# Pair 3 of step 0 written straight into the tiles of x, step 0's scores in 64-key blocks, GpSimd as a choice for the weights' high parts

## The chip, the cores and the metric

The kernel runs on one core of one Trainium2 chip. The metric is device time in microseconds (us) of one launch; three runs of the kernel before gave 467.01, 467.27 and 467.72, so its median is 467.27 us.

## What is computed

A gated linear attention over 768 positions, 4 batches and 8 heads of 48 values, followed by a two-layer network with a piecewise gate. Cut to what matters:

```python
for t in range(S):
    state = f[t] * state + k[t] (outer) v[t]
    y[t] = q[t] @ state
x = y of all heads, as (B * S, 384)
h = x @ w_in                    # 384 -> 2048
g = where(h >= 1, h, where(h <= -1, 0, (h + 1) ** 2 / 4))
out = g @ w_out                 # 2048 -> 384
```

## The kernel before

The 768 positions are cut into six steps of 128. Heads go in four pairs, and a pair's two heads lie on partitions 0 to 47 and 64 to 111. Per step the attention of the four pairs fills three tiles of x (128 rows by 512 columns, four batches of 128 positions): tile t holds pair t on rows 0 to 47 and 64 to 111, and sixteen of pair 3's values of each head on rows 48 to 63 and 112 to 127. x is kept as a high and a low part in the type fp32r. The network takes a step's x in 16 units; a unit is 9 matmuls of 512 columns into `ph` (L267; `mm_in`), an elementwise chain on ScalarE and VectorE (L270, L273, L278, L934, L281), and 9 matmuls of 512 columns into `po` (L288; `mm_out`). That makes 96 units, u = 0 to 95. The attention of later steps is put between the units: `TURNS` and `VISITS` say after which u a pair is turned, scored, begun and finished, and `AFTER` puts step 0's key transposes (`turn`, `transpose_tensor`, L685) and states after units 0 to 3.

Weights come in as 32 pieces of 128 x 384. `split_piece` (L376 to L393) makes bits on ScalarE (L385), joins them on VectorE (L387), copies the high part (L390 names the choice: ScalarE, and for the first 16 pieces VectorE too), and subtracts it to get the low part on VectorE (L391).

TensorE's instructions stand in the order in which the code adds them. For ScalarE, VectorE, GpSimd and SyncE a planner (`Plan.order`, L98) lists the operations from costs (`COST`) and due times; where `either` gives two engines, it takes the one that it finds free first.

Step 0 has no state before it and is the start of the kernel. Its order is the list `START`: gates of the pairs (L500), their scores (L614), masks (L630), the values times masked scores (`heads`, L851). Pair 3 goes first, in two halves (numbers 3 and 7). In the kernel before, `last` computes pair 3's outputs into a bank of their own (`last_heads`, L853), ScalarE and VectorE round them into a high and a low part (L705, L706, tiles `ghi` and `glo`), and `tile` t brings sixteen rows of each head to rows 48 and 112 of tile t by two matmuls with a selection matrix (L881, `select` made by GpSimd, L844 to L846). `heads` t adds pair t. After that the bank is rounded into x, and `unit_0` (L905) is the first unit's first layer, one third per tile of x. Before START, warm-up matmuls run on zeros (L355).

The scores of step 0 are 128 x 128 per head and batch, all keys by all queries, and a 128 x 128 mask of zeros and ones takes away the later keys. The keys stand in reverse order. The scores of later steps are already taken in 64-key blocks (`scores_of_two`, L666, four 64 x 64 parts of the array at a time).

Of the kernel before, what the change touches and what calls it, by code (L numbers as in the profile page):

```python
# [51 lines left out]
KB_FIRST, KB_LATER, KB_L = 1.75, 0.82, 1.0  # L52
COST = dict(half_dve=350, half_gates=460, half_scores=570, half_log=330, half_sig=330, half_gate=350, gates=870, log=500, mm=227, scores=1100, heads=950, own=1200, tile=680, both=1090, begin=480, before=930, part=560, states=850, parts=830, turn=350, first=110, last=95,
# [4 lines left out]
TURNS = {4: 4, 5: 4, 6: 10, 7: 10, 8: 17, 9: 17, 10: 22, 11: 22, 12: 28, 13: 28, 14: 37, 15: 37, 16: 40, 17: 40, 18: 46, 19: 46, 20: 60, 21: 60, 22: 70, 23: 70}  # L58
VISITS = {4: (4, 5, 6), 6: (10, 11, 13), 8: (21, 22, 26), 10: (26, 27, 29), 12: (28, 32, 37), 14: (37, 39, 40), 16: (40, 45, 47), 18: (47, 60, 61), 20: (61, 69, 70), 22: (70, 75, 77)}
# [3 lines left out]
BY_PRODUCT, ON_EITHER = (), 16  # L63
# [121 lines left out]
def gla_moe(ctx: ExitStack, tc: tile.TileContext, ff, ld, kd, kqd, f0, vv, vl, wd, gates, values, headsd, out):  # L185
# [36 lines left out]
    mask_z = const.tile([C, C + 1], F32, name="mask")  # L222
# [6 lines left out]
    row_ok, least_ok = mask[0:1], ok[0:1, 1:2]  # L229
# [82 lines left out]
    def make_mask():  # L312
        nc.gpsimd.memset(mask_z, 1.0)
        nc.gpsimd.affine_select(out=mask_z, in_=mask_z, pattern=[[1, C + 1]], compare_op=ALU.is_ge, fill=0.0, base=-C, channel_multiplier=1)
# [38 lines left out]
    def warm_first():  # L353
        for cols in WARM:
            nc.tensor.matmul(ph[1][:, 0:cols], zeros, zeros[:, 0:128].rearrange("p (o c) -> p o c", o=1).broadcast_to([128, max(cols // 128, 1), 128])[:, :, 0:min(cols, 128)], start=True, stop=True)  # L355
# [20 lines left out]
    def split_piece(k):  # L376
# [13 lines left out]
        h = plan.either(dict(ACT="part_hi", DVE="cast_384") if k < ON_EITHER else dict(ACT="part_hi"), lambda copy: copy(hi, val), v)  # L390
# [46 lines left out]
    ready = {"mask": set_mask, "sel": add("POOL", 700, make_ident), "mask_t": add("POOL", 600, make_mask_t, set_mask)}  # L437
# [24 lines left out]
    def first_loads(n):  # L462
# [13 lines left out]
        if parts == 1:  # L476
            c["lk"] = 2 * [dma(kq[n][:, 0:2 * N], kd[n], KB_LATER * 512)]
        else:
            c["lk"] = [dma(kq[n][:, a], kd[n, :, a], KB_FIRST * 256) for a in (slice(0, N), slice(N, 2 * N))]
# [122 lines left out]
    def scores(n):  # L602
# [6 lines left out]
        c["held"].append([bank(b) for b in ((5, 6), (3, 4), (5, 2), (3, 4), (5, 6))[n + k * (NP - n)]])  # L609
# [8 lines left out]
    am_of = [am[2:4], kn, am[0:2], am[0:2]]  # L618

    def masks(n):  # L620
# [7 lines left out]
        for h, (b, ps, _) in enumerate(c["held"][k]):  # L628
            t = am_of[n][h]
            o = vec("dve" if parts == 1 else "half_dve", lambda t=t, ps=ps: nc.vector.tensor_tensor(  # L630
                out=t[:, some], in0=ps[:, some], in1=mask.rearrange("u (o t) -> u o t", o=1).broadcast_to([C, B // parts, C]), op=ALU.mult),
                c["sc"][k], ready["mask"], att[3]["y"] if n == 2 else [])
            c["am"].append(o)
            banks[b][:] = [o]
# [43 lines left out]
    def transpose_tensor(n, at=None):  # L678
# [30 lines left out]

    def rounded_by_tensor(b, yf, hi, lo, y):  # L710
        eh = sca("round", lambda: nc.scalar.copy(hi, yf), y)
        banks[b] = [eh]
        return [eh, None]

    def rest(t):

        k, yf, hi, lo = rests[t]
        x = att[NP - 1]["x"] if t == NT else x_of[0, t]
        rows = yf.shape[0]
        o = add("PE", COST["mm"], lambda: nc.tensor.matmul(yf, minus[:rows, :rows], hi, start=False, stop=True), x[0], ready["minus"])  # L720
        x[1] = sca("round", lambda: nc.scalar.copy(lo, yf), o)
        banks[k].append(x[1])
# [112 lines left out]
    sel = glo[0][:R, 0:NT * C].rearrange("r (t c) -> r t c", t=NT)  # L835
    minus = glo[0][:, NT * C:]
    y_last = ghi[1][:R], glo[1][:R]
    rests = {}

    def negative():  # L840
        nc.gpsimd.tensor_scalar(out=minus, in0=ident, scalar1=-1.0, scalar2=None, op0=ALU.mult)

    def select():
        nc.gpsimd.memset(sel.bitcast(F32), 0.0)  # L844
        for t in range(NT):
            nc.gpsimd.tensor_copy(out=sel[:, t].rearrange("r (e c) -> r e c", e=2)[:, :, D:], in_=ident[:R].rearrange("r (e c) -> r e c", e=2)[:, :, 16 * t:16 * t + 16])  # L846

    def heads(n, ps, start, stop):
        for m in range(B):
            for e in range(2):  # L850
                nc.tensor.matmul(ps[64 * e:64 * e + D, m], value(2 * n + e, m), am_of[n][e][:, m], start=start and m == 0, stop=stop and m == B - 1)  # L851

    def last_heads(n):  # L853
        c = att[n]
        b, ps, held = bank(1)
        c["y"] = add("PE", "heads", lambda: heads(n, ps, True, True), c["am"], c["lv"], held)
        if NT in BY_PRODUCT:
            rests[NT] = b, wide(ps)[:R], *y_last
            c["x"] = rounded_by_tensor(*rests[NT], c["y"])
        else:  # L860
            c["x"] = rounded(b, wide(ps)[:R], *y_last, c["y"], None)
# [3 lines left out]
    def half_tile(t, own):  # L865
# [3 lines left out]
        b, ps, held = bank((0, 3, 1)[t])  # L869

        def clear_bank():
            nc.tensor.matmul(wide(ps), zeros, zeros.rearrange("p (o c) -> p o c", o=1).broadcast_to([128, 4, 128]), start=True, stop=False)

        def emit_own():
            if done is None:
                clear_bank()
            heads(t, ps, False, done is not None)

        def emit_last():
            for k in range(2):  # L880
                nc.tensor.matmul(wide(ps), sel[:, t], y_last[k], start=done is None and k == 0, stop=done is not None and k == 1)  # L881

        if own:
            o = c["y"] = add("PE", "own" if done is None else "heads", emit_own, c["am"], c["lv"], held, set_zeros, done)
# [309 lines left out]
```

## Time and profile before

| | |
|---|---|
| median of three runs | 467.27 us |
| the profiled execution | 466.99 us |
| its span, first to last instruction | 465.3 us |
| TensorE busy / VectorE / ScalarE / GpSimd | 458.6 / 345.2 / 299.2 / 24.4 us |
| granted TensorE clock | 1.00 over the whole span |

The span begins with the first instruction and leaves out 1.7 us of the execution's time. In the views, PE is TensorE, DVE VectorE, ACT ScalarE and POOL GpSimd; a line such as L685 is a line of the kernel printed above. An fp32 matmul shows as two instructions (two passes), an fp32 transpose or an fp32r matmul as one. A busy time counts an instruction until its modelled end, so on TensorE, where one begins before the last has ended, the step from start to start is the time that counts.

### The profile page before, as it was taken

How to read it: one execution, taken by the hardware profiler on the slowest of the kernel's cores; microseconds unless marked ns; L12 is line 12 of the kernel's file. 1: busy time of each engine (PE TensorE's matmuls, PEld its weight loads, DVE VectorE, ACT ScalarE, POOL GpSimd, SP SyncE). 2: the span in 40 equal slices, each digit the busy share in tenths (PEclk: the TensorE clock that was granted, in tenths of full speed). 3: DMA queues.
4: the chain of work that ended last, by engine and by line, in shares of the span. 5: the costliest groups of instructions: out<-in, count | busy, mean ns of one | idle time of the engine just before them, and what ended most of it. 6: DMA issues, size and time to landing. Idle time of an engine off the chain costs nothing.

```text
span 465.3 us, 10971 instructions
## 1 busy us (share of the span) xinstructions
PE 458.6 (99%) x4496; PEld 376.2 (81%) x4496; DVE 345.2 (74%) x691; ACT 299.2 (64%) x557; POOL 24.4 (5%) x81
## 2 busy tenths in 40 slices
PE   8999999999999999999999999999999999999996
PEld 5788888888888888888888888888878888888884
DVE  3989987989999998988987887677566755533332
ACT  7799899899574766577576647446536454654443
POOL 4102000010010201000020000000000000000000
PEclk9999999999999999999999999999999999999999
DMA  7888684563023153054236313245412224300001
GB/s 272 296 269 263 210 269 138 187 178 90 4 67 125 49 137 104 1 194 127 59 85 215 117 58 92 68 136 143 132 57 69 71 85 117 102 1 0 1 0 71
DMA packets 21716, 54.19 MB, mean 116 GB/s; under 512 B 3424, under 2 KB 4192, under 8 KB 21664
## 3 DMA queue, kind: packets, MB, share of 16 engines
q1 hardware_dynamic: 21520, 53.37, 36.9%
q8 instruction: 36, 0.59, 0.5%
q10 hardware_dynamic: 144, 0.10, 0.1%
q14 instruction: 16, 0.13, 0.1%
HBM read 44.80 MB, written 4.72 MB: 106 GB/s over the span
## 4 chain that ended last, share of the span: by engine, by line
PE 96%; DMA 2%; SPq 1%; DVE 1%; issue 0%; ACT 0%; DVEq 0%
PE po L288 43%; PE ph L267 42%; PE pa L733 2%; PE pa L755 2%; PE ph L666 2%; DMA kq<-in_k 2%; PE pa L804 1%; SPq L294 1%; PE pa L685 1%; PE pa L666 1%; PE ph L905 0%; PE ph L804 0%; PE pa L783 0%; DVE kq L513 0%; DVE am L630 0%
## 5 line engine op out<-in xcount | busy, mean ns | idle before, releaser
L267 PE MATMUL ph<-x,w_hi 128*128 128x512 f32 x570 | 146.4, 389 | 0.0
L270 ACT ACTIVATE act<-ph,half 128x512 f32<-128x512 f32 x96 | 65.9, 687 | 95.4 <-PE ph L267 94.7
L267 PEld LDWEIGHTS ph<-x,w_hi 128*128 128x128 f32 x570 | 106.9, 188 | 22.2
L278 DVE SCALAR_TENSOR_TENSOR act<-ph,act 128x512 f32<-128x512 f32 x96 | 66.1, 689 | 64.4 <-ACT act L273 63.6
L934 ACT CAST ghi<-act 128x512 fp32r<-128x512 f32 x96 | 59.4, 619 | 50.0 <-DVE act L278 49.7
L288 PE MATMUL po<-ghi,w_hi 128*128 128x512 f32 x288 | 86.2, 401 | 0.0
L288 PE MATMUL po<-ghi,w_lo 128*128 128x512 f32 x288 | 83.2, 390 | 0.0
L288 PE MATMUL po<-glo,w_hi 128*128 128x512 f32 x288 | 82.9, 389 | 0.0
L281 DVE TENSOR_TENSOR glo<-act,ghi 128x512 fp32r<-128x512 f32 x96 | 66.2, 690 | 22.1 <-ACT ghi L934 20.2
L267 PE MATMUL ph<-x,w_lo 128*128 128x512 f32 x285 | 81.6, 389 | 0.0
L700 DVE STREAM_TRANSPOSE kn<-kq 32x128 f32<-32x128 f32 x224 | 67.6, 302 | 3.6
L288 PEld LDWEIGHTS po<-ghi,w_lo 128*128 128x128 f32 x288 | 54.1, 188 | 11.6
L288 PEld LDWEIGHTS po<-glo,w_hi 128*128 128x128 f32 x288 | 54.1, 188 | 11.5
L273 ACT ACTIVATE act<-act 128x512 f32<-128x512 f32 x96 | 60.7, 632 | 2.8
L267 PEld LDWEIGHTS ph<-x,w_lo 128*128 128x128 f32 x285 | 53.5, 188 | 11.1
L288 PEld LDWEIGHTS po<-ghi,w_hi 128*128 128x128 f32 x288 | 52.0, 188 | 11.2 <-ACT ghi L934 0.3
L401 DVE TENSOR_REDUCE ok<-raw 128x1 f32<-128x384 f32 x64 | 33.1, 544 | 2.5 <-DMA raw<-in_w 2.5
L391 DVE TENSOR_TENSOR w_lo<-bits,w_hi 128x384 fp32r<-128x384 f32 x32 | 17.7, 554 | 4.4 <-ACT w_hi L390 3.8
L545 POOL COPY end<-w 128x4 f32<-128x4 f32 x15 | 5.2, 349 | 287.5 <-ACT w L544 287.5
L385 ACT ACTIVATE bits<-raw,top_of 128x384 uint32<-128x384 fp8e4 x32 | 20.1, 645 | 0.0
L596 ACT ACTIVATE sd<-sd,kq 112x48 f32<-112x48 f32 x80 | 19.7, 323 | 0.0
L541 DVE TENSOR_TENSOR_SCAN w<-rec,f 128x512 f32<-128x512 f32 x15 | 18.3, 1219 | 0.8 <-ACT f L540 0.6
(139 smaller groups left out, 382.8 us busy)
## 6 DMA issues: line engine op xcount, KB each, us to landing
raw<-in_w SPq DMA_DIRECT2D x32, 384.0 KB, 3.1
raw<-in_w SPq DMA_DIRECT2D x32, 383.6 KB, 3.6
kq<-in_kq SPq DMA_DIRECT2D x15, 512.0 KB, 4.8
v<-in_v SPq DMA_DIRECT2D x12, 384.0 KB, 3.8
out_y<-raw SPq DMA_DIRECT2D x18, 256.0 KB, 2.5
f<-in_f SPq DMA_DIRECT2D x15, 256.5 KB, 2.9
kq<-kq SPq DMA_DIRECT2D x30, 64.2 KB, 2.6
x<-y SPq DMA_DIRECT2D x30, 64.0 KB, 2.3
```

Of the source, the lines that this page charges most:

```text
L267: nc.tensor.matmul(ps, w_in(w_hi if high else w_lo, j, kt), xt[:, kt, t], start=(n == 0), stop=(n == 8))
L270: nc.scalar.activation(a, ps, AF.Relu, bias=half, scale=0.5)
L273: nc.scalar.activation(a, a, AF.Square)
L278: nc.vector.scalar_tensor_tensor(out=a, in0=ps, scalar=1.0, in1=a, op0=ALU.max, op1=ALU.min)
L281: nc.vector.tensor_tensor(out=lo, in0=a, in1=hi.bitcast(F32), op=ALU.subtract)
L288: nc.tensor.matmul(po[e], w_out(part, j, e), g, start=(j == 0 and n == 0), stop=(j == NJ - 1 and n == 2))
L385: m = sca("bits", lambda: nc.scalar.activation(t, top, AF.Abs, bias=top_of, scale=2.0 ** 30), loaded, made[k - 4] if k >= 4 else None, set ...
L401: seen.append(vec("join", lambda z=z, op=op: nc.vector.tensor_reduce(out=ok[:, 1 + NG + z + c:2 + NG + z + c], in_=words_of(raw[2])[1].bit ...
L541: s1 = vec("scan", lambda: nc.vector.tensor_tensor_scan(out=wide(w), data0=wide(rec), data1=ft[:, N:0:-1], initial=0.0, op0=ALU.mult, op1= ...
L596: nc.scalar.activation(ds[:, at + b * D:at + (b + 1) * D], state[:, p * B + b], AF.Copy, scale=pf[:R, b:b + 1])
L700: nc.vector.transpose(kn[n % 2][to:to + 32, ::-1, r:r + 32], src[:, :, u:u + 32])
L934: o = g["hi"] = sca("copy", lambda: nc.scalar.copy(hi, a), o, unit_out.get(u - 2))
```

## The change

- START has no `last`. `tile` t now multiplies the masked scores of pair 3 with 64 neighbouring columns of the values, such that the last sixteen are the wanted ones, and writes all 64 rows of each half of the bank; `heads` t then overwrites the first 48 of each 64. The selection matrix, the rounding of pair 3 and the clearing of a bank are gone.
- `scores` of step 0 makes, for each batch, the first 64 positions' keys by all 128 queries and the later 64 keys by the later 64 queries. For odd batches the two key halves change places in the bank, so that the long and the short product alternate on the column halves of the array. The value rows of odd batches are exchanged on the host, the mask gets a second version (`make_odd`), and the parts of the banks that are not written hold zeros from the warm-up.
- The key transposes of step 0 follow: for odd batches the transpose of 128 key positions becomes two products of 64 key positions with the identity.
- Pieces 4 and later of the weights may have their high part copied by ScalarE or GpSimd; pieces 0 to 3 by ScalarE or VectorE.
- The order of START, the places in TURNS and VISITS, two costs of scores and the assumed size factor of one load are new.

```diff
-TURNS = {4: 4, 5: 4, 6: 10, 7: 10, 8: 17, 9: 17, 10: 22, 11: 22, ...}
-VISITS = {4: (4, 5, 6), 6: (10, 11, 13), 8: (21, 22, 26), ...}
-START = (("gates", 3), ("gates", 7), ("gates", 0), ("scores", 3), ("scores", 7), ("gates", 2), ("mask", 3), ("mask", 7), ("gates", 1),
-         ("last", 3), ("scores", 0), ("scores", 1), ("tile", 0), ("mask", 0), ("mask", 1), ("heads", 0), ("scores", 2), ("mask", 2), ("tile", 2), ("tile", 1), ("heads", 1), ("heads", 2), ("unit", 0), ("unit", 1), ("unit", 2))
+TURNS = {4: 4, 5: 4, 6: 9, 7: 9, 8: 14, 9: 14, 10: 21, 11: 21, ...}
+VISITS = {4: (4, 5, 7), 6: (9, 10, 11), 8: (17, 21, 24), ...}
+START = (("gates", 3), ("gates", 7), ("gates", 0), ("scores", 3), ("scores", 7), ("mask", 3), ("mask", 7), ("gates", 1), ("gates", 2),
+         ("tile", 2), ("scores", 0), ("tile", 1), ("tile", 0), ("scores", 1), ("mask", 0), ("mask", 1), ("heads", 0), ("scores", 2), ("mask", 2), ("heads", 1), ("heads", 2), ("unit", 0), ("unit", 1), ("unit", 2))
...
+    def make_odd():
+        odd = mask[:, C:]
+        nc.gpsimd.memset(odd[0:T, T:], 1.0)
+        nc.gpsimd.memset(odd[T:, 0:T], 0.0)
+        nc.gpsimd.tensor_copy(out=odd[0:T, 0:T], in_=mask[0:T, T:C])
+        nc.gpsimd.tensor_copy(out=odd[T:, T:], in_=mask[T:, 0:T])
...
-        h = plan.either(dict(ACT="part_hi", DVE="cast_384") if k < ON_EITHER else dict(ACT="part_hi"), lambda copy: copy(hi, val), v)
+        h = plan.either(dict(ACT="part_hi", POOL="pool_hi") if k >= 4 else dict(ACT="part_hi", DVE="cast_384"), lambda copy: copy(hi, val), v)
...
             for m in range(k * B // parts, (k + 1) * B // parts):
-                for (a, z), (_, ps, _) in zip(HEADS, c["held"][k]):
-                    nc.tensor.matmul(ps[:, m], key(n, m)[a:z], query(n, m)[a:z], start=True, stop=True)
+                for half, since in ((1, 0), (0, T)):
+                    at = T * (half ^ m & 1)
+                    for (a, z), (_, ps, _) in zip(HEADS, c["held"][k]):
+                        nc.tensor.matmul(ps[at:at + T, m, since:], key(n, m)[a:z, T * half:T * half + T], query(n, m)[a:z, since:], start=True, stop=True)
...
             for m in range(B):
-                nc.tensor.transpose(ps[:, m, :R], key(p, m)[:R], ident[:R, :R])
+                if i == 0 and m % 2:
+                    for k in range(2):
+                        nc.tensor.matmul(ps[T * (1 - k):T * (2 - k), m, :R], key(p, m)[:R, T * k:T * k + T], ident[:R, :R], start=True, stop=True)
+                else:
+                    nc.tensor.transpose(ps[:, m, :R], key(p, m)[:R], ident[:R, :R])
...
-            for k in range(2):
-                nc.tensor.matmul(wide(ps), sel[:, t], y_last[k], start=done is None and k == 0, stop=done is not None and k == 1)
+            for m in range(B):
+                for e in range(2):
+                    to = (4 * (B + m) + 1 + 2 * e) * D + 16 * (t + 1)
+                    nc.tensor.matmul(ps[64 * e:64 * e + 64, m], v_all[:, to - 64:to], am_of[NP - 1][e][:, m], start=m == 0, stop=m == B - 1)
...
+    vv[0, :, :, 1::2] = np.roll(vv[0, :, :, 1::2], T, axis=1)
```

## Rows read from the trace of the kernel before

**Rows 1.** The page, parts 1 and 2: busy time per engine, TensorE's granted clock.
```profile
PE 458.6 (99%) x4496; PEld 376.2 (81%) x4496; DVE 345.2 (74%) x691; ACT 299.2 (64%) x557; POOL 24.4 (5%) x81
...
PEclk9999999999999999999999999999999999999999
```
**Rows 2.** Chain that ended last, 20 to 33 us: start, us, what, count.
```profile
20.42 2.30 PE ph L905 x9
22.72 0.39 PE pa L685 x4
23.11 0.38 PE po L685 x4
23.49 2.08 PE ph L267 x9
...
30.74 0.77 PE pa L685 x8
```
**Rows 3.** The same chain, 50 to 60 us, around one visit.
```profile
50.56 2.04 PE ph L267 x9
52.60 1.04 PE pa L755 x64
53.64 0.45 PE pa L733 x32
54.09 2.27 PE po L288 x9
56.36 2.04 PE ph L267 x9
```
**Rows 4.** The same chain, the load that the start waits for.
```profile
4.68 7.12 DMA kq<-in_k
```
**Rows 5.** Timeline of VectorE in the start: start, us, operation, idle before.
```profile
11.89 0.69 DVE L512 TENSOR_TENSOR kq<-kq,raw 112x512 f32<-112x512 f32 x1 [0.92 <-DMA kq<-in_k]
12.50 0.68 DVE L513 TENSOR_TENSOR kq<-kq,raw 112x512 f32<-112x512 f32 x1
13.10 0.68 DVE L706 TENSOR_TENSOR glo<-pa,ghi 112x512 fp32r<-112x512 f32 x1
13.70 0.68 DVE L630 TENSOR_TENSOR am<-po,mask 128x512 f32<-128x512 f32 x1
...
15.49 0.69 DVE L513 TENSOR_TENSOR kq<-kq,sd 112x512 f32<-112x512 f32 x1
...
18.36 0.68 DVE L630 TENSOR_TENSOR am<-pa,mask 128x512 f32<-128x512 f32 x1
```
**Rows 6.** Timeline of TensorE in the start.
```profile
10.68 1.08 PE L851 MATMUL pa<-am,v 128*48 128x128 f32 x16 [0.36 <-DMA v<-in_v]
...
13.23 1.16 PE L614 MATMUL po<-kq 48*128 48x128 f32 x16 [0.39 <-DVE kq L513]
...
17.32 0.50 PE L881 MATMUL pa<-ghi,glo 112*128 112x512 f32 x1
...
18.47 1.08 PE L851 MATMUL po<-kn,v 128*48 128x128 f32 x16
19.38 1.04 PE L851 MATMUL pa<-am,v 128*48 128x128 f32 x16
20.35 0.50 PE L905 MATMUL ph<-x,w_lo 128*128 128x512 f32 x1
```
**Rows 7.** Groups by line and shape: the copies of high parts, and GpSimd's nearest work.
```profile
L390 ACT CAST w_hi<-bits 128x384 fp32r<-128x384 f32 x26 | 13.1, 505 | 1.6 <-DVE bits L387 1.6
...
L390 DVE CAST w_hi<-bits 128x384 fp32r<-128x384 f32 x6 | 2.2, 359 | 0.2
...
L841 POOL TENSOR_SCALAR glo<-ident 128x128 fp32r<-128x128 f32 x1 | 0.5, 532 | 0.1
...
L846 POOL CAST glo<-ident 112x32 fp32r<-112x32 f32 x3 | 0.5, 209 | 0.1
```
**Rows 8.** Timelines of GpSimd and VectorE at 153 us.
```profile
153.82 1.52 POOL L545 COPY end<-w 128x4 f32<-128x4 f32 x1 [17.49 <-ACT w L544]
...
154.01 0.69 DVE L546 TENSOR_TENSOR kq<-kq,w 128x512 f32<-128x512 f32 x1
154.61 0.69 DVE L547 TENSOR_TENSOR kq<-kq,f 128x512 f32<-128x512 f32 x1
```
**Rows 9.** Busy time of each engine by stretch (columns as named), 20 to 100 us.
```profile
20.00:100.00 80.00, 80.00 (x903) 65.64 (x900) 70.46 (x127) 73.43 (x148) 3.71 (x10) 1.00 0.69 218
```
**Rows 10.** Timeline, 43 to 45 us: a weight piece's high part and its first use.
```profile
43.74 0.52 ACT L390 CAST w_hi<-bits 128x384 fp32r<-128x384 f32 x1
...
44.78 1.07 PE L267 MATMUL ph<-x,w_hi 128*128 128x512 f32 x4
```

More of the change, by code (lines that the diff above doesn't have):

```diff
@@ L51 @@
 HOP, LANDING, PER_KB, NEAR, ADDING, PATIENCE, FLAG_BY = 200, 2200, 3.0, 3500, 1500, 0, 60000
-KB_FIRST, KB_LATER, KB_L = 1.75, 0.82, 1.0
-COST = dict(half_dve=350, half_gates=460, half_scores=570, half_log=330, half_sig=330, half_gate=350, gates=870, log=500, mm=227, scores=1100, heads=950, own=1200, tile=680, both=1090, begin=480, before=930, part=560, states=850, parts=830, turn=350, first=110, last=95,
+KB_FIRST, KB_NEXT, KB_LATER, KB_L = 1.75, 1.21, 0.82, 1.0
+COST = dict(pool_hi=800, half_dve=350, half_gates=460, half_scores=440, half_log=330, half_sig=330, half_gate=350, gates=870, log=500, mm=227, scores=840, heads=950, own=1200, tile=680, both=1090, begin=480, before=930, part=560, states=850, parts=830, turn=350, first=110, last=95,
@@ L221, in gla_moe @@
     w_lo = const.tile([128, NW, W], F32R, name="w_lo")
-    mask_z = const.tile([C, C + 1], F32, name="mask")
+    mask_z = const.tile([C, 2 * C + 1], F32, name="mask")
     mask = mask_z[:, 1:]
@@ L312, in make_mask @@
     def make_mask():
-        nc.gpsimd.memset(mask_z, 1.0)
-        nc.gpsimd.affine_select(out=mask_z, in_=mask_z, pattern=[[1, C + 1]], compare_op=ALU.is_ge, fill=0.0, base=-C, channel_multiplier=1)
+        causal = mask_z[:, 0:C + 1]
+        nc.gpsimd.memset(causal, 1.0)
+        nc.gpsimd.affine_select(out=causal, in_=causal, pattern=[[1, C + 1]], compare_op=ALU.is_ge, fill=0.0, base=-C, channel_multiplier=1)
     def make_ident():
@@ L353, in warm_first @@
     def warm_first():
-        for cols in WARM:
-            nc.tensor.matmul(ph[1][:, 0:cols], zeros, zeros[:, 0:128].rearrange("p (o c) -> p o c", o=1).broadcast_to([128, max(cols // 128, 1), 128])[:, :, 0:min(cols, 128)], start=True, stop=True)
+        for k, cols in enumerate(WARM):
+            nc.tensor.matmul((po + ph)[k if k < 4 else 4][:, 0:cols], zeros, zeros[:, 0:128].rearrange("p (o c) -> p o c", o=1).broadcast_to([128, max(cols // 128, 1), 128])[:, :, 0:min(cols, 128)], start=True, stop=True)
     add("PE", 3700, warm_first, set_zeros)
@@ L630, in masks @@
             o = vec("dve" if parts == 1 else "half_dve", lambda t=t, ps=ps: nc.vector.tensor_tensor(
-                out=t[:, some], in0=ps[:, some], in1=mask.rearrange("u (o t) -> u o t", o=1).broadcast_to([C, B // parts, C]), op=ALU.mult),
-                c["sc"][k], ready["mask"], att[3]["y"] if n == 2 else [])
+                out=by_two(t[:, some]), in0=by_two(ps[:, some]), in1=mask.rearrange("u (o t) -> u o t", o=1).broadcast_to([C, B // 2 // parts, 2 * C]), op=ALU.mult),
+                c["sc"][k], ready["odd"], att[3]["y"] if n == 2 else [])
             c["am"].append(o)
@@ L708, in rounded @@
         return [eh, el]
[L710 to L722, printed above, removed]
     def attended(n, other):
@@ L831, in states_by_parts, with heads @@
         freed(k, held, o, z)
[L835 to L848, printed above, removed]
+    def heads(n, ps):
         for m in range(B):
             for e in range(2):
[L851 to L861, printed above, removed]
+                nc.tensor.matmul(ps[64 * e:64 * e + D, m], value(2 * n + e, m), am_of[n][e][:, m], start=m == 0, stop=m == B - 1)
     half_of = {}
@@ L868, in half_tile @@
         done = half_of.get(t)
[L869 to L877, printed above, removed]
+        b, ps, held = bank((0, 2, 1)[t])
         def emit_last():
[L880 to L881 removed]
+            for m in range(B):
+                for e in range(2):
+                    to = (4 * (B + m) + 1 + 2 * e) * D + 16 * (t + 1)
+                    nc.tensor.matmul(ps[64 * e:64 * e + 64, m], v_all[:, to - 64:to], am_of[NP - 1][e][:, m], start=m == 0, stop=m == B - 1)
         if own:
[L884 to L890 removed]
+            o = c["y"] = add("PE", "heads", lambda: heads(t, ps), c["am"], c["lv"], done)
+            x_of[0, t] = rounded(b, wide(ps), x[0][:, t, 0], x[0][:, t, 1], o, None)
+        else:
+            o = add("PE", "heads", emit_last, d["am"], d["lv"], held)
+            d.setdefault("y", []).append(o)
+            half_of[t] = o
     gs, left = {}, {}
@@ L995, in gla_moe @@
         att[n]["lv"] = att[n - 1]["lv"]
-    ready["ident"] = ready["sel"]
-    ready["sel"] = add("POOL", 1200, select, ready["ident"])
-    ready["minus"] = add("POOL", 1500, negative, ready["ident"])
-    work = dict(gates=first_gates, mask=masks, scores=scores, last=last_heads, heads=lambda t: half_tile(t, True), tile=lambda t: half_tile(t, False), rest=rest, unit=unit_0,
+    work = dict(gates=first_gates, mask=masks, scores=scores, heads=lambda t: half_tile(t, True), tile=lambda t: half_tile(t, False), unit=unit_0,
                 turn=lambda n: transpose_tensor(n, {0: 1, 1: 5}.get(n)), states=lambda n: states(n))
@@ L1161 @@
     f0 = f0.reshape(128, NG)
-    vv = np.ascontiguousarray(v[:, heads].reshape(B, 2, 4, NI, C, D)[:, :, :, :, ::-1].transpose(3, 1, 4, 0, 2, 5))
+    vv = np.array(v[:, heads].reshape(B, 2, 4, NI, C, D)[:, :, :, :, ::-1].transpose(3, 1, 4, 0, 2, 5), order="C")
+    vv[0, :, :, 1::2] = np.roll(vv[0, :, :, 1::2], T, axis=1)
     w = moe_w_in.reshape(H, D, DF)
```

22 lines of the change are left out of this document (9 added, 13 removed).

## The prediction

> **What bounds the kernel now.** I read the page's busy times first, then the chain of work that ended last, then the timelines of the stretch where that chain isn't TensorE. TensorE is busy for 99% of the span, at the full clock of 2.4 GHz throughout [rows 1]. In the chain it works without a gap from 20.42 us on: unit follows unit in 2.04 us for nine matmuls, and what stands between them is attention [rows 2, 3]. So the span has two parts. After 20.42 us only the amount of TensorE's work counts, changes of its array's shape included. Before 20.42 us it waits, and what counts is how soon the first unit can begin.
>
> That start hangs on one load and then on VectorE. The keys and queries of pair 1 leave SyncE at 4.68 us and land 7.12 us later, at 11.79 [rows 4]. VectorE has stood idle for 0.92 us by then, and from there it works back to back, one 512-column operation each 0.60 us: gating pair 1, the rounding of pair 3 (13.10), masks of pair 0, gating pair 2 (ending at 16.18), masks of pairs 1 and 2, the last ending at 19.04 [rows 5]. TensorE follows it: scores of pair 2 after 16.18, selection matmuls for two tiles (from 17.32), heads 1 at 18.47, heads 2 at 19.38, first unit at 20.35 [rows 6].
>
> **The start, part by part.** Removed from the path: the rounding of pair 3, 0.60 us of VectorE right after the awaited load [rows 5], its copy on ScalarE, and six selection matmuls. Added: `tile` three times instead of `last` once, each eight products of two passes like a `heads`, which takes 0.9 us from start to next start (18.47 to 19.38) [rows 6]. The scores get three quarters of their columns, since the long and short blocks fill the two column halves in turn: 1.16 us in the view less a pipeline end, 0.85 of it streaming [rows 6], so about 0.2 less for each.
>
> I lay the new order on the old landings. The loads are issued in nearly the same order, since what decides their due times keeps its order; only the gate logits of pairs 1 and 2 change places. `tile` 2 needs the values, as `last` did, so it starts at 10.68. Scores 0 then run from 11.7, tile 1 from 12.55, tile 0 from 13.4, scores 1 from 14.4 to 15.15, heads 0 from 15.25, scores 2 from 16.25 to 17.0, heads 1 from 17.2 to 18.07. VectorE from 11.89: two operations of pair 1's gates, two masks of pair 0 (until 14.3), two gates of pair 2 (15.5), two masks of pair 1 (16.7), the joining of a weight piece in the gap, two masks of pair 2 from 17.25, ending at 18.53. Heads 2 waits for that, runs from 18.6 to 19.5, and the first unit starts at 19.6 instead of 20.35: **0.75 us sooner**. If VectorE is no obstacle, TensorE's own sum gives 19.05, a gain of 1.3; if the planner puts another operation or two ahead of a mask, it gives 0 to 0.15. I take 0.75, because rows 5 show VectorE without a gap in this stretch. Next late would be the mask of pair 2, as now.
>
> Of work at no cost: GpSimd makes the second mask instead of the selection matrix, of about as much work, and has nothing else to do then (24.4 us of work in all [rows 1]); if it came late, the masks of pair 3 would wait, ahead of the load at 11.79. The warm-up has the same columns, only other banks. Units read the same x.
>
> **The key transposes.** This term isn't hidden by anything, for it lies after 20.42. Now eight transposes of two pairs take 0.77 us, one each 0.096 us, and the unit behind them takes 2.08 instead of 2.04 [rows 2]: they use the whole array, as units do. In the change, two of the four transposes of each of the four pairs become two products on 64 columns of the array each. Each is fp32 with two passes; the halves run beside each other, as the heads e = 0 and 1 do (16 passes of 128 columns in 0.9 us, [rows 6]), so an odd batch streams 0.19 us instead of 0.096. That is 8 x 0.095 = 0.76 us. Then the array changes its shape twice for each odd batch, since even and odd ones alternate. Rows 3 price one such change and back: the first attention group takes 1.04 us for 64 passes where the next takes 0.45 for 32, so 0.14 us to go in; the group of nine behind takes 2.27 instead of 2.04, so 0.23 to come out, of which 0.04 is there after transposes too [rows 2, 3]. I take 0.14 + 0.19 = 0.33 for each of eight. In sum 8 x (0.095 + 0.33) = **3.4 us added**. Bounds: 0.76 if a change between small products costs nothing, 8 x (0.285 + 0.37) = 5.2 if the halves don't overlap either.
>
> **GpSimd and the weights.** Pieces 4 to 31 may have their high part copied by GpSimd, and as ScalarE is busy for 73.4 of the 80 us from 20 to 100 [rows 9], the planner will give it most. That frees some 28 x 0.45 us of ScalarE and a little of VectorE, which is worth nothing while TensorE has no gap. Its price is not in the trace. The nearest rows are a cast of 32 columns in 0.21 us and an operation on 128 in 0.53 [rows 7], which go on to 1.4 us for 384; the columns of the plain copies would give 0.9. ScalarE's takes 0.505. A piece is made just ahead of its use: one is copied by 44.26 and used at 44.78 [rows 10]. Against a delay of 0.4 to 0.9 stand that 0.5 and the 2.65 us by which TensorE is later from unit 2 on, so I cost it at nothing; this cover is gone if the transposes turn out free, and then a few tenths for each tight piece come back. The upper end is a rival below.
>
> The new places: the visits fall on 24 different units before and 24 after, so the changes of shape there stay the same in number, and with no gap on TensorE their place is free.
>
> **Sum.** The profiled execution took 466.99: -0.75 + 3.4 gives 469.64. The median of the three runs is 0.28 above it: **469.9 us**. The terms' bounds give 466.99 - 1.3 + 0.76 = 466.5 and 467 + 5.2 = 472.2 on the profiled execution.
>
> **The rivals.** First, **the transposes cost only their columns**: TensorE takes the changes of shape in its stride because no wait stands there, and only 0.76 us is added. For it: no row has whole-array and half-array products alternate so finely. Against it: 2.27 follows every visit I looked at [rows 3]. With the start at TensorE's own limit this gives 467.27 - 1.3 + 0.76 = 466.7, not slower. It decides from 0.07 us per change and back: below that, 8 x (0.095 + 0.07) = 1.3 is paid by the start. Chance 0.17. A start much sooner still (masks of pair 0 and gates of pair 2 in the wait for the load), with cheap transposes, would give 466 or below; chance 0.08.
>
> Second, **GpSimd and VectorE block each other**. A copy of four elements on GpSimd took 1.52 us while VectorE ran operations with two inputs from SBUF back to back, VectorE's own taking their usual 0.69 [rows 8]. VectorE makes the low part in its order and would stand waiting for a copy that it held up itself. VectorE has 80 - 70.5 = 9.5 us free from 20 to 100 [rows 9], so it decides at about 9.5 / 28 = 0.34 us lost per copy; at 0.6, some 7 us are lost on VectorE beyond that and perhaps 5 reach TensorE: 469.9 + 3 to 5, near 474. Chance 0.12. The Trainium skill, SBUF — State Buffer, section "SBUF: two separate sides", says that GpSimd and a VectorE operation with two SBUF inputs share one pair of ports, that whichever starts first has it for its whole instruction, and that the other is blocked. By that rule a 1 us copy would also hold VectorE, up to 28 us in all; the trace agrees for the one direction, GpSimd held, and no row shows the other.
>
> Third, the start doesn't move, because another wait (the values of pairs 0 and 1, the second such load) or the planner's order on VectorE takes the place: 466.99 + 3.4 + 0.28 = 470.7. I count it with the forecast.
>
> **How the numbers follow.** Forecast with its variants (start 0 to 1.3 sooner, transposes 2 to 5): 0.63, which is slower. GpSimd blocking: 0.12, slower. Cheap transposes: 0.17, within 0.2% (0.93 us, about what a measurement of this kernel can tell from no change). A much sooner start: 0.08, faster. So faster 0.08, same 0.17, slower 0.75. The range from 466.6 to 472.2 holds the forecast's bounds and most of the first rival, and leaves out the blocking and the sooner start.
>
> **What would show it.** Right, if the chain has the first unit (L905) at 19.3 to 19.9 us, if two step-0 turns take 1.5 to 1.9 us instead of 0.77 with the half-array products in separate lumps, and if nine-matmul groups still follow at 2.04 and 2.27. Wrong, if the turns take under 1.2 us, if the first unit is under 19.0 or over 20.3, or if TensorE's groups show idle time released by VectorE's low parts or GpSimd's copies between 25 and 100 us; GpSimd's busy time there divided by its copies gives their price.

## The result and the profile after

The changed kernel takes 470.29 us (median of six runs, 469.81 to 470.88) beside 467.35 us for the kernel before on the same chip (six runs, 467.01 to 468.14): a ratio of 1.006, with a 95% interval from 1.0047 to 1.0073. It is slower by 2.9 us. The profiled execution took 470.04 us with a span of 468.3, against 466.99 and 465.3.

In the page of after, the first line of part 1 answers to [rows 1]. TensorE is busy for the same 99%, with 116 more matmuls in the records; its granted clock is at the upper level in all 40 slices, as before.

```profile
PE 461.8 (99%) x4612; PEld 377.2 (81%) x4612; DVE 347.0 (74%) x688; ACT 295.7 (63%) x545; POOL 32.0 (7%) x93
```

The chain that ended last, of the kernel after, from the last work of the start to the second unit (it answers to [rows 2]; columns: start, us, what, count; L841 is `heads`, L878 the first unit's first layer, L700 the half-array products and L702 the whole transposes of step 0's turns):

```profile
18.15 0.21 PE ph L358
18.37 1.26 PE pa L841 x16
19.62 2.30 PE ph L878 x9
21.93 0.10 PE pa L702
22.02 0.34 PE pa L700 x4
22.36 0.24 PE pa L702
22.61 0.34 PE pa L700 x4
...
24.13 2.27 PE ph L266 x9
...
29.52 2.04 PE ph L266 x9
```

The first unit begins 0.80 us sooner (19.62 against 20.42). Then two turns take 2.20 us (21.93 to 24.13) where they took 0.77, and the unit behind them 2.27 instead of 2.08. A whole transpose that begins the turns shows 0.10, one behind half-array products 0.24: that is the way back, 0.14 to 0.15. An odd batch (four instructions, two products of two passes) takes 0.34 where, standing among others of its kind, it takes 0.19 (shown with the sorted batches below): about 0.15 to go in. The other two turns, at 31.56, look the same.

So that kernels can be compared whatever their start, I took the starts of the units from the timeline of TensorE, counted from the start of the first unit, and the end of the span counted from the last matmul's start (us). "Unit 3" lies behind all turns of step 0, "unit 95" is the last.

| kernel | first unit at | unit 1 | unit 3 | unit 5 | unit 95 | end after last matmul |
|---|---|---|---|---|---|---|
| before | 20.35 | 2.91 | 13.09 | 24.43 | 432.03 | 4.75 |
| after | 19.55 | 4.50 | 16.32 | 27.65 | 435.57 | 5.05 |
| difference | -0.80 | +1.59 | +3.23 | +3.22 | +3.54 | +0.30 |

The sum is -0.80 + 3.54 + 0.30 = +3.04, the 3.0 us of the span. From unit 5 to unit 95 only 0.3 is added: 0.4 at one place, a turn of a later step at 69 us, less 0.1 that comes back later. In the timeline of TensorE (start, us, operation, idle before and its releaser):

```profile
69.58 0.57 PE L702 MATMUL pa<-ident,kq 112*128 112x112 f32 x4 [0.20 <-DVE w_lo L398]
```

The view counts idle time from the modelled end of the work before, so it shows 0.20 of the 0.4. It names VectorE's low part, which ended at 69.51, but the records speak for a load. The keys of this turn (pair 3) are put in place by a transfer `kq<-kq` (L296), issued at 64.00 and landed at 69.38, and the turn begins 0.20 us behind that. When the same kernel was run again, the transfer landed at 69.78 and the turn began at 69.98, while that low part ended only at 70.08. With all copies on GpSimd it landed at 67.68, and the turn didn't wait.

The last 0.30 is the landing of the last output, which came between 4.75 and 5.96 us after the last matmul in the fourteen profiles of this case. The two lowest values are those of the kernel before and of the split alone in it; the changed kernel has 5.05 here and 4.85 when run again, so two executions of one kernel differ by 0.20 there.

GpSimd got 13 of the 28 copies that it might have had. From the groups by line and shape, of GpSimd and of ScalarE (they answer to [rows 7]), and the busy times from 20 to 100 us (they answer to [rows 9]):

```profile
L397 POOL CAST w_hi<-bits 128x384 fp32r<-128x384 f32 x13 | 9.5, 734 | 44.3 <-DVE bits L394 44.3
...
L397 ACT CAST w_hi<-bits 128x384 fp32r<-128x384 f32 x19 | 9.6, 509 | 1.5 <-DVE bits L394 1.3
```
```profile
20.00:100.00 80.00, 79.80 (x907) 63.79 (x906) 71.13 (x122) 70.34 (x136) 14.10 (x25) 1.00 0.69 215
```

ScalarE lost 3.1 us of work in that stretch (73.43 to 70.34), VectorE gained 0.7, and TensorE still has next to no idle time.

### The profile page after: what moved, and what is told of

Same layout as the page of the kernel before. It is cut to its first block, busy times and chain, and to the rows that moved or that the text cites. A ratio compares the mean times of both kernels' runs of the same rounds, so it can differ in the third digit from the quotient of the medians.

```text
span 468.3 us, 11210 instructions
## 1 busy us (share of the span) xinstructions
PE 461.8 (99%) x4612; PEld 377.2 (81%) x4612; DVE 347.0 (74%) x688; ACT 295.7 (63%) x545; POOL 32.0 (7%) x93
## 4 chain that ended last, share of the span: by engine, by line
PE 95%; ACT 1%; DVE 1%; DMA 1%; issue 0%; SPq 0%; DVEq 0%
PE po L287 42%; PE ph L266 41%; PE pa L736 2%; PE pa L758 2%; PE ph L679 2%; DMA kq<-in_k 1%; PE pa L807 1%; PE pa L841 1%; PE pa L855 1%; PE po L623 1%; PE pa L702 1%; PE pa L679 1%; PE ph L878 0%; PE pa L507 0%; PE pa L700 0%; PE ph L807 0%
## 5 line engine op out<-in xcount | busy, mean ns | idle before, releaser
L280 DVE TENSOR_TENSOR glo<-act,ghi 128x512 fp32r<-128x512 f32 x96 | 67.4, 703 | 22.4 <-ACT ghi L907 20.6
```

The costliest lines, as they stand in the source:

```text
L280: nc.vector.tensor_tensor(out=lo, in0=a, in1=hi.bitcast(F32), op=ALU.subtract)
```

## The experiments

Each kernel was timed against the kernel before on the same chip. Differences of single places are taken from the profiles, by the table's measure.

**The split transposes alone, in the kernel before.** Nothing else of the change is made.

```diff
-                nc.tensor.transpose(ps[:, m, :R], key(p, m)[:R], ident[:R, :R])
+                if i == 0 and m % 2:
+                    for k in range(2):
+                        nc.tensor.matmul(ps[T * k:T * k + T, m, :R], key(p, m)[:R, T * k:T * k + T], ident[:R, :R], start=True, stop=True)
+                else:
+                    nc.tensor.transpose(ps[:, m, :R], key(p, m)[:R], ident[:R, :R])
```

> The kernel before with one thing alone: step 0's key transposes of odd batches as two half-array products. Theory (the changes of the array's shape and the extra columns make the loss): 8 odd batches at about 0.40 us, so 3.2 us more, 470.6 against 467.35; the first unit stays at 20.4 us, and two turns take 2.2 us instead of 0.77. Rival (the loss of the change comes from GpSimd's copies or the new places): 467.4, at most 0.8 us more for the extra columns.

Measured: 470.91 us against 467.69, ratio 1.007 (1.0053 to 1.0087). Unit 3 comes 16.30 us behind the first unit, 3.21 later than in the kernel before. The chain shows the same steps as that of after (here L687 are the half-array products, L689 the whole transposes):

```profile
23.13 0.10 PE pa L689
23.23 0.34 PE pa L687 x4
23.57 0.24 PE pa L689
...
25.34 2.27 PE ph L267 x9
```

These eight split transposes alone make the loss: 3.2 us on TensorE, and 3.2 on the median.

**The batches sorted.** In the changed kernel, the whole transposes of two pairs stand together, and the half-array ones too. The work is the same, only the number of changes of shape falls.

```diff
-            for m in range(B):
+            for m in (range(B), (0, 2, 1, 3), (1, 3, 0, 2))[0 if i else 1 + n % 2]:
```

> The changed kernel with the batches of each two turns sorted as 0, 2, 1, 3 and 1, 3, 0, 2, so that the four half-array batches stand together: one change of shape and back for two turns instead of four. Theory (0.31 us per change and back, 0.095 us of columns per odd batch): two turns take 0.92 us less, in sum 1.85 us less, 468.4 against 470.3. Rival (the half-array products themselves are that slow, wherever they stand): no difference, 470.3.

Measured: 468.47 us against 467.69, ratio 1.0019 (1.001 to 1.0028); the changed kernel itself has 1.006. Unit 3 comes 14.41 us behind the first unit instead of 16.32, so 1.91 is saved. The chain:

```profile
22.82 0.19 PE pa L702 x2
23.02 0.53 PE pa L700 x8
23.55 0.38 PE po L700 x8
23.93 0.34 PE po L702 x2
24.27 2.08 PE ph L266 x9
```

Two turns now take 1.45 us, and the unit behind them 2.08: together 0.66 more than with whole transposes, where the changed kernel pays 1.60. Both pay the same columns, four odd batches of 0.095, which is 0.38. What is left is 1.22 for four changes and back, 0.31 each, and 0.28 for the single one here. So the shape change is the larger part of the price, 2.5 us of the 3.2 for all eight. The rival, half-array products that are slow wherever they stand, falls: in a lump four odd batches' products add only their columns (two batches in 0.38).

**Whole transposes, the halves exchanged by the copy out.** The transposes are as before, and the copy of step 0's turned keys becomes three, of which two exchange the key halves of the odd batches.

```diff
-                if i == 0 and m % 2:
...
+                nc.tensor.transpose(ps[:, m, :R], key(p, m)[:R], ident[:R, :R])
...
+                copy(kn[n % 2][:, 0::2, :R], ps[:, 0::2, :R])
+                copy(kn[n % 2][0:T, 1::2, :R], ps[T:C, 1::2, :R])
+                copy(kn[n % 2][T:C, 1::2, :R], ps[0:T, 1::2, :R])
```

> The changed kernel with whole transposes for all batches; the copies out of the bank, three instead of one for each pair of step 0, put the halves of odd batches in their places. Theory: TensorE gets back 3.2 us, two turns take 0.77 us again, the first unit stays at 19.55 us: 467.1, so 0.2 to 0.6 us below the kernel before if the earlier start is a gain by itself. Rival (the pieces of weights or the states come late once TensorE is that much sooner, so that the start's gain goes into a wait in units 0 to 3): 467.4 or above, with idle time on TensorE before the states.

Measured: 468.48 us against 467.69, ratio 1.0026 (1.0014 to 1.0038). The turns are back at their old cost: unit 3 comes 13.05 us behind the first unit. But a weight's high part is now late by the time that TensorE has come sooner. From the timelines of ScalarE and TensorE:

```profile
38.64 0.49 ACT L397 CAST w_hi<-bits 128x384 fp32r<-128x384 f32 x1
...
39.19 1.20 PE L266 MATMUL ph<-x,w_hi 128*128 128x512 f32 x4 [0.55 <-ACT w_hi L397]
```

In the kernel after, a copy begins at 38.70 too, and TensorE doesn't wait there. Unit 5 is 25.49 us behind the first unit, where the kernel before has 24.43, so 1.06 is lost again, which is more than the start has gained. The rival held in kind, a weight that is late, though behind the states and not ahead of them.

**The same, with all copies of high parts from piece 4 on given to GpSimd.**

```diff
-        h = plan.either(dict(ACT="part_hi", POOL="pool_hi") if k >= 4 else ...
+        h = plan.either(dict(POOL="pool_hi") if k >= 4 else ...
```

> Whole transposes and exchange by the copies, as in the run that had a late weight piece at 38 us, and all high parts from piece 4 on by GpSimd. Theory (ScalarE was what made the piece late): no gap at 38 us, the start's 0.75 us stay, 0.5 to 0.8 us below the kernel before. Rival (the pieces stay late, now by GpSimd or the loads): a gap of 0.5 us or more in units 2 to 6, no faster than the kernel before.

Measured: 468.49 us against 467.42, ratio 1.0023 (1.0013 to 1.0033). The rival held, and the waits only move: unit 5 comes 25.73 us behind the first unit, 1.30 later than in the kernel before. Ahead of unit 5 the view has one wait of 0.4 us, put down to VectorE's low part; the rest is in shorter waits, which it leaves out:

```profile
PE po L287 <- DVE w_lo L398: 0.4, 1, 0.4
```

**The same again, with the old places of TURNS and VISITS.** The diff sets the two dictionaries back to the lines taken out in the change.

> The same with the places of the kernel before. Theory (with GpSimd making the high parts the plan has no gap at either set of places): equal to the run before it within 0.3 us. Rival (the new places belong to the new plan): 0.5 us or more slower than it, with a gap at one of the visits.

Measured: 471.28 us against 467.42, ratio 1.0094 (1.0068 to 1.0121). The rival held. With the old places TensorE falls behind the kernel before in the stretches from 128, 159 and 201 us, by 1.0, 0.5 and 1.4; unit 95 comes 436.29 us behind the first, 2.5 later than with the new places (433.78). The profiled execution of this kernel was 3.2 us above its median, with a late first unit (22.58), so only its places are used here.

**The exchange left out.** The turns are whole and the copy out is the single old one, all else is as in the kernel after.

```diff
-                if i == 0 and m % 2:
-                    for k in range(2):
...
-                else:
-                    nc.tensor.transpose(ps[:, m, :R], key(p, m)[:R], ident[:R, :R])
+                nc.tensor.transpose(ps[:, m, :R], key(p, m)[:R], ident[:R, :R])
```

> The changed kernel with whole transposes and one copy out of the bank as before. Left out: the exchange of the key halves of step 0's odd batches, so the states after step 0 are of other numbers; work and waits are otherwise the kernel's. Theory (the late weight piece of the two runs with three copies comes from the two additional copies on ScalarE and VectorE): no gap on TensorE up to unit 5, which begins 24.4 us after the first unit, 0.5 to 0.8 us below the kernel before. Rival (the weights are made no sooner, so a sooner start has to wait for them): unit 5 begins 25.0 us or more after the first unit, and the time is within 0.4 us of the kernel before.

Measured: 467.13 us against 467.33, ratio 1.0002 (0.9992 to 1.0012). The chain has the early start and the old turns, and later the copy of the outputs before the last transfer:

```profile
19.63 2.30 PE ph L874 x9
21.93 0.39 PE pa L698 x4
22.31 0.38 PE po L698 x4
22.70 2.08 PE ph L266 x9
...
460.14 0.58 ACT raw L933
```

No weight is late: unit 5 is 24.43 and unit 95 is 432.02 us behind the first unit, as in the kernel before. This kernel and the kernel after differ in the split transposes alone, and unit 95 comes 3.55 us sooner here, 3.23 of it by unit 3: with the split alone in the kernel before, that shows from both sides what the loss is. It also shows that the waits of the three experiments above came with the two added copies and the plan around them, not with an earlier TensorE alone. TensorE ends 0.80 sooner (the output's copy begins at 460.14 instead of 460.95), yet the median is only 0.2 lower, which is not clear of the noise and misses the 0.5 to 0.8 expected. In the one profile the last output landed 0.92 us later behind the last matmul (5.67 against 4.75), which takes up the gain. The three output transfers took 2.50, 2.52 and 2.99 us there, and 2.17 to 2.19 in the kernel before; in the changed kernel run again they took 2.17 to 2.28, so the longer ones don't belong to the new start as such. One profile doesn't settle whether they always take the gain; this stays open.

**Whole scores.** In the kernel after, step 0's scores, mask and transposes are as before, with no exchange at all; pair 3 still goes straight into the tiles.

```diff
-                for half, since in ((1, 0), (0, T)):
-                    at = T * (half ^ m & 1)
...
+                for (a, z), (_, ps, _) in zip(HEADS, c["held"][k]):
+                    nc.tensor.matmul(ps[:, m], key(n, m)[a:z], query(n, m)[a:z], start=True, stop=True)
...
-    vv[0, :, :, 1::2] = np.roll(vv[0, :, :, 1::2], T, axis=1)
```

> The changed kernel with step 0's scores whole again, 128 keys by 128 queries, and so without exchanged halves, second mask or split transposes; pair 3 still goes straight into x. Theory (TensorE's own work from the first tile to the last scores sets the start, and each scores costs 0.17 us more): first unit at 20.0 us, 467.5. Rival (VectorE's chain of gates and masks sets the start, the blocks are worth nothing): first unit at 19.6 us, 467.1.

Measured: 467.59 us against 467.69, ratio 1.0003 (0.9992 to 1.0014). The whole loss is gone, and the start's gain too. The values landed later on this chip (the first product of pair 3 began at 11.12 instead of 10.64), so I compare from that product on. From it to the first unit the kernel before takes 9.68 us (10.68 to 20.35 [rows 6]), this one 9.65 (11.12 to 20.77), and the kernel after 8.91. The timeline of TensorE in the kernel after, for that:

```profile
10.64 1.09 PE L855 MATMUL pa<-am,v 128*64 128x128 f32 x16
...
14.40 0.90 PE L623 MATMUL po<-kq 48*64 48x128 f32 x32
15.23 1.08 PE L841 MATMUL pa<-am,v 128*48 128x128 f32 x16
...
17.07 1.08 PE L841 MATMUL pa<-kn,v 128*48 128x128 f32 x16
18.08 0.28 PE L358 MATMUL ph<-zeros 128*128 128x256 bf16 x1
18.30 1.33 PE L841 MATMUL pa<-am,v 128*48 128x128 f32 x16
19.55 0.50 PE L878 MATMUL ph<-x,w_lo 128*128 128x512 f32 x1
```

The scores of pair 1 take 0.83 us from start to next start (14.40 to 15.23); whole ones take 1.09 in the experiment (15.13 to 16.22). Three times 0.26 is 0.78, about the 0.74 between the two kernels. Writing pair 3 straight into the tiles alone buys nothing: the scores of pair 2 begin 6.11 us behind the first product instead of 5.55, because of the three `tile` groups, and from there to the first unit it takes 3.54 instead of 4.12. The other half alone, blocks in the kernel before, wasn't run, so the experiment doesn't say that the blocks would bring 0.74 without the other edit.

**The changed kernel again**, on the chip of the next three experiments:

> The changed kernel as it is, on the same chip as the next three. Theory: first unit 8.9 us after the first tile's matmuls begin, two turns 2.2 us, 2.6 to 3.0 us above the kernel before. The wait of 0.39 us of the turn of pair 3 in step 1 (at 69 us in the profile after) is a late landing and comes and goes: 0 or 0.4.

Measured: 470.86 us against 467.58, ratio 1.0065 (1.004 to 1.0091), 3.3 us above the kernel before where 2.6 to 3.0 was expected. The first unit begins 9.10 us behind the first tile's matmuls (seven of the eleven profiles of this start have 8.91), two turns take 2.20 us, and the turn at 69 us loses 0.2, between the two values expected.

**The old places in the changed kernel.** TURNS and VISITS are set back, nothing else.

> The changed kernel with the TURNS and VISITS of the kernel before. Theory (with no gap on TensorE the places are free): within 0.4 us of the changed kernel. Rival (the new places bring waits): 0.5 to 1 us faster than it.

Measured: 473.13 us against 467.58, ratio 1.0115 (1.0093 to 1.0137), 2.3 us over the changed kernel: neither the theory nor the rival held. Unit 95 comes 1.55 later behind the first unit (437.22 against 435.67 in the changed kernel run beside it), and in two places the plan has put matmuls on zeros into gaps that it expected; whether TensorE would really have waited so long there isn't shown. One of the two, in the timeline of TensorE:

```profile
159.22 0.82 PE L353 MATMUL po<-zeros 128*128 128x512 bf16 x3
```

Such matmuls stand nowhere behind the start of the kernel after. The other stands at 375.69. The profiled execution also has a later landing of the last output (5.96 against 4.85 us behind the last matmul).

**No copies on GpSimd.** The choice of engines for the high parts is the old one.

```diff
-        h = plan.either(dict(ACT="part_hi", POOL="pool_hi") if k >= 4 else dict(ACT="part_hi", DVE="cast_384"), ...
+        h = plan.either(dict(ACT="part_hi", DVE="cast_384") if k < 16 else dict(ACT="part_hi"), ...
```

> The changed kernel with the high parts copied as before, by ScalarE or, for the first 16 pieces, VectorE. Theory (GpSimd's 13 copies cost and bring nothing while TensorE is later by 2.4 us): within 0.4 us of the changed kernel. Rival (GpSimd and VectorE block each other to TensorE's loss): 1 us or more faster.

Measured: 474.66 us against 467.58, ratio 1.0149 (1.0126 to 1.0173), 3.8 us over the changed kernel; again neither held. Unit 95 comes 438.66 us behind the first, 3.0 later. The largest gap is the same turn at 70 us: its transfer `kq<-kq` was issued at 66.48 instead of 64.00 and landed at 71.70, 0.24 before the turn (the view names another load). About 1.2 us more are four matmuls on zeros that the plan put at 105 us, and 0.4 more is lost at about 149 us, where masked scores are late. From the timeline of TensorE, and the busy times from 20 to 100 us:

```profile
71.94 0.57 PE L702 MATMUL pa<-ident,kq 112*128 112x112 f32 x4 [1.05 <-DMA raw<-in_w]
```
```profile
20.00:100.00 80.00, 78.95 (x909) 62.62 (x905) 66.19 (x119) 69.75 (x140) 3.74 (x9) 1.00 0.65 203
```

**All 28 copies on GpSimd.** The diff is that of the run "with all copies given to GpSimd", made in the kernel after.

> The changed kernel with all 28 high parts of pieces 4 to 31 on GpSimd. Theory: a copy takes 0.50 us alone and 0.8 beside VectorE, VectorE's operations with two inputs lose up to 0.3 each, some 6 to 8 us in sum, which its idle time until 100 us takes in: at most 0.5 us slower than the changed kernel. Rival (the loss reaches TensorE): 3 to 5 us slower, with TensorE waiting for low parts between 25 and 100 us.

Measured: 470.36 us against 467.58, ratio 1.0057 (1.0037 to 1.0077), 0.5 below the changed kernel and within the spread of four runs each; the theory held. From the groups, and the busy times from 20 to 100 us:

```profile
L397 POOL CAST w_hi<-bits 128x384 fp32r<-128x384 f32 x28 | 19.9, 717 | 51.7 <-DVE bits L394 51.7
```
```profile
20.00:100.00 80.00, 80.00 (x907) 64.12 (x908) 72.17 (x121) 65.16 (x125) 25.83 (x40) 1.00 0.70 218
```

The view shows no idle time of TensorE behind the start, not even at 69 us, although GpSimd does more than twice the copies.

**Old places and old engines together**, both of the last diffs in the kernel after.

> The changed kernel with both the places and the choice of engines for high parts of the kernel before. Theory (places and engines have to fit each other; the loss of the change itself is the split transposes): TensorE has under 1 us of gaps and fillers after the first unit, 470.3 to 471.2. Rival (the changed start needs GpSimd's help with the weights, wherever the visits are): 472 or more, with TensorE waiting between 60 and 110 us.

Measured: 473.54 us against 467.42, ratio 1.013 (1.0109 to 1.0151). Unit 95 comes 438.39 us behind the first, 2.7 later than in the changed kernel, so the rival's time came. Of its waits, at 69.7, 130.8 and 379 us, only the first lies where the rival put it, and at 161 us the plan has three matmuls on zeros. TensorE's waits behind the start:

```profile
PE pa L736 <- DVE am L685: 0.6, 1, 0.6
...
PE po L287 <- ACT ghi L907: 0.3, 1, 0.3
...
PE po L287 <- ACT w_hi L397: 0.3, 1, 0.3
```

In the kernel before the two old parts leave TensorE no gap, and with the split transposes alone they cost 0.45 (unit 95 at 435.69, less 3.21 for the turns, against 432.03). With the new start they don't fit. Which of its shifted operations on ScalarE and VectorE makes the difference wasn't tried.

## Why the prediction was right, and where its reasons weren't

**The key transposes** were the largest term and held: 3.4 us forecast, 3.23 measured in the kernel after and 3.21 with the split alone. The columns were right (eight times 0.095 us, from halves that run beside each other). The change of shape and back was put at 0.33 from [rows 3]; the two kernels with and without sorting give 0.31 and 0.28. Its parts lie a little otherwise, about 0.15 to go in and 0.14 to come out where another attention product follows, and 0.19 more than after whole transposes in the unit behind the last one (2.27 against 2.08).

**The first rival**, that only columns are paid, needed less than 0.07 us per change and falls with that.

**The start** had the right size, 0.75 forecast and 0.80 measured, and the steps that I laid out came near: scores of pair 2 at 16.24 (16.25 in the forecast), heads 2 at 18.30 (18.6), the first unit at 19.55 (19.6). The last masks, in the timeline of VectorE in the kernel after (it answers to [rows 5]):

```profile
16.67 0.55 DVE L394 SCALAR_TENSOR_TENSOR bits<-raw,bits 128x384 uint32<-128x384 uint32 x1
17.20 0.69 DVE L643 TENSOR_TENSOR am<-po,mask 128x512 f32<-128x512 f32 x1
17.81 0.68 DVE L643 TENSOR_TENSOR am<-ph,mask 128x512 f32<-128x512 f32 x1
```

They end at 18.49, as forecast (18.53), and heads 2 waits for them, as forecast. With 0.91 us for heads 1 from 17.07 and 0.97 for heads 2 (their steps in [rows 6]), the first unit would begin at 18.95 without that wait (19.05 in the forecast) instead of 19.55; the matmul on zeros at 18.08 only fills part of it.

The step that failed is where the gain was booked: "Removed from the path: the rounding of pair 3, 0.60 us of VectorE right after the awaited load". With rounding and selection gone but whole scores, the start gains nothing (9.65 against 9.68); with the 64-key blocks added it gains 0.74 more, 0.26 for each of three scores where I took 0.2. Yet the removal isn't idle. In the kernel before, the chain comes to the scores of pair 2 from VectorE's gate:

```profile
15.49 0.70 DVE kq L513
...
16.23 0.37 PE po L614
```

In the kernel after, that gate ends at 15.56, and TensorE's own work sets when these scores begin, at 16.24. So in the kernel before, shorter scores ahead of that gate would have met a wait, and only the 0.26 of pair 2's would be left, an estimate from these rows that no run tested. The two edits seem to need each other; I had laid out one sum with both in it, and that its size came out doesn't confirm the share given to either.

**GpSimd's copies.** The step "the planner will give it most" failed: it gave 13 of 28. The price of a copy was too high: 0.9 to 1.4 us was extrapolated from smaller operations, and a copy that nothing holds up takes 0.50. The cover for late pieces was put too early, too: it was to be 2.65 us from unit 2 on, but only two of the four turns are done by then, and TensorE is 0.8 us later at unit 2 and 2.4 from unit 3 on. Costing the copies at nothing was wrong in its reason, since "worth nothing while TensorE has no gap" holds only as long as the plan around them has no gap either: without them the new plan loses 3.0 us on TensorE, 1.2 of it in matmuls on zeros that the plan itself put in. Since they come together with the plan that needs them, the sum was not hurt.

**The blocking rival** decided at 0.34 us lost on VectorE per copy, and would have cost 3 to 5 us. VectorE lost less: in the kernel after, eight of its operations that met a copy took 2.1 us more in all than such operations take otherwise, 0.16 per copy, and with all 28 copies fourteen took 3.8 us more, 0.14 per copy, without idle time on TensorE. The copies themselves took 0.23 longer on average (734 ns against 0.50). The blocking itself is there, in both directions. From the timelines of GpSimd and VectorE in the kernel after:

```profile
35.57 0.90 POOL L397 CAST w_hi<-bits 128x384 fp32r<-128x384 f32 x1 [0.75 <-DVE bits L394]
...
89.64 0.51 POOL L397 CAST w_hi<-bits 128x384 fp32r<-128x384 f32 x1 [7.31 <-DVE bits L394]
...
95.56 1.37 POOL L397 CAST w_hi<-bits 128x384 fp32r<-128x384 f32 x1 [3.37 <-DVE bits L394]
```
```profile
35.42 0.68 DVE L553 TENSOR_TENSOR kq<-kq,w 128x512 f32<-128x512 f32 x1
36.02 0.99 DVE L280 TENSOR_TENSOR glo<-act,ghi 128x512 fp32r<-128x512 f32 x1
...
89.80 0.89 DVE L280 TENSOR_TENSOR glo<-act,ghi 128x512 fp32r<-128x512 f32 x1 [0.22 <-ACT ghi L907]
...
95.42 1.22 DVE L548 TENSOR_TENSOR_SCAN w<-rec,f 128x512 f32<-128x512 f32 x1
```

The copy at 35.57 begins inside L553 and takes 0.90; the next operation with two inputs, L280, begins inside the copy and takes 0.99 where its mean over the kernel is 0.70. The copy at 89.64 begins ahead of L280 and keeps its 0.51, and L280 takes 0.89. So the copies of 0.50 are not all alone: most of them began first. The Trainium skill, SBUF — State Buffer, section "SBUF: two separate sides", says that whichever of the two starts first holds the shared ports for its whole instruction, and that the other is blocked. The trace now agrees in the direction that no row before showed, VectorE held by GpSimd, at 0.2 to 0.3 us for an operation that met a copy. What the rival had wrong is the price of a meeting, and that VectorE had the time for it.

**The new places** were called free: "the visits fall on 24 different units before and 24 after ... their place is free". That failed as a reason. Their changes of shape do cost the same (with whole transposes unit 95 comes at 432.03 with the old places and at 432.02 with the new), but the places also decide when ScalarE and VectorE must have the attention's operations done. The old places cost the changed kernel some 1.5 us on TensorE, in gaps and in matmuls on zeros. The forecast was not hurt, because the new places suit the new plan, which I had not shown.

**The third rival**, a start that doesn't move, falls with the 0.80, and so does a much sooner start with cheap transposes. What the sum did not hold is 0.31 between units 5 and 95, from the turn at 69 us (0.4 there in this profile, 0.2 when the kernel was run again), and 0.30 at the last transfer. With the start 0.05 and the transposes 0.17 below their terms, that makes the 0.4 by which the profiled execution (470.04) lies above the sum (469.64); that the errors lay on both sides is luck.

**The signs.** The first unit (19.62 in the chain, 19.3 to 19.9 expected) and the groups of nine at 2.04 and 2.27 came as named. The range for two turns, 1.5 to 1.9 us, was a slip: the prediction's own terms give 0.77 + 4 x 0.425, less the 0.19 paid in the unit behind, which is 2.28, and 2.20 was measured; 1.70 is only what is added. One sign of being wrong showed up in small, idle time of TensorE put down to VectorE's low part (0.20 at 69 us); as laid out above, it goes back to the landing of a transfer.

## What to carry to other kernels

When TensorE has no gap, it can pay to sort small products by the part of the array that they use: here the same eight split transposes cost 3.2 us one by one between whole ones and 1.3 us in lumps. Before a second benefit is booked for an edit that stands next to another, one should ask by which of the two it would be lost; here the one edit alone brought nothing, both together brought 0.77 us of the start, and the other alone wasn't run. Places and engine choices of a planned kernel are tuned together, and a part that "costs nothing" in one plan costs 2 to 4 us when it is put into another.

## What the runs showed of the hardware that was not expected

GpSimd copied 128 x 384 from fp32 to fp32r in 0.50 to 0.51 us in 7 of 13 copies, as fast as ScalarE (0.509). The other six began while a VectorE operation ran, and took 0.77 to 0.90, or 1.37 beside a scan. In eight cases a VectorE operation that began inside a copy took 0.2 to 0.3 longer.

Two batches of half-array fp32 products in a lump took 0.38 us, 0.19 for a batch and twice the 0.096 of one whole transpose; a change between half and whole took about 0.15 each way, on a TensorE that had no wait there in which to hide it.
